# Two attention schedules in one kernel: blocks of 64 tokens for the second sequence, chunks two by two for the first

## The chip, the cores and the metric

The kernel runs on one core of a Trainium2 chip. The metric is device time in microseconds (us) of one execution. Five engines run their own instruction streams and wait for each other by semaphores: PE (TensorE, matmul; PEld is its loading of weights), DVE (VectorE), ACT (ScalarE), POOL (GpSimd) and SP (SyncE), whose queue issues nearly all DMAs.

## The reference

Three stages follow each other: a decayed linear attention, a dense layer with a gelu, and a layer of 8 routed experts.

```python
for b in range(nb):                      # attention: blocks of 64 tokens, head_dim 64
    intra = einsum('bhic,bhjc->bhij', qb, kb) * Dmask      # lam ** (i - j), i >= j
    intra = einsum('bhij,bhjd->bhid', intra, vb)
    inter = einsum('bhid,bhde->bhie', qb * lam_pow, kv_state)
    out[:, :, sl] = intra + inter
    kv_state = lam_block * kv_state + einsum('bhsd,bhse->bhde', kb * rev_pow, vb)
# dense layer on x [1536, 512]
h = x @ w_in                             # w_in [512, 2048]
y = (h * sigmoid(1.702 * h)) @ w_out     # w_out [2048, 512]
# experts
e = argmax(norm(y) @ norm(emb).T / tau)  # one of 8 experts a token, gate = its softmax
out = gate * (relu(y @ w1[e]) @ w2[e])
```

There are 2 sequences of 768 tokens with 8 heads. The size of the attention's blocks does not change what is computed: any block length gives the same sum, split in another way into a part within the block (intra) and a part through the carried state (inter).

## The kernel before

Attention goes in chunks of 128 tokens, six to a sequence (ci 0 to 5 for the first sequence, 6 to 11 for the second), with the 8 heads as 4 pairs, so that two heads of 64 dimensions fill 128 partitions. A chunk has these steps: scores (L228, 8 fp32 matmuls that contract 64 partitions, half of the array each), sm (scores times the mask of decays, DVE L245), kd and qd (k and q scaled by powers of lam, POOL L252 and L258), intra (L279, outputs of 64 columns of the array, half of the array each), inter (L298 for the first sequence, in quarters of the array with the states; L291 for the second, whole array with the state tiles of a pair laid out as a block diagonal, `blocks`), pk (L310, the new part of the state), sd (the old state scaled, ACT L320), state (DVE L329), and the output x as a high part (xh, ACT L342) and a rest (xl, DVE L345). Every fp32 matmul shows as two records in the trace, each with its own loading of weights.

The dense layer runs over 16 hidden blocks f of 128 columns, twice: `emit_moe1_first` for the first sequence, `emit_moe1_last` for the second. A block's weights come as raw 64-bit words, are decoded by three DVE operations (L368, L371, L374) and split into a high half (ACT L386) and a low half (DVE L387); `decode_w(f, kind)` and `split_w(g, f, kind)` are these steps, kind 0 for w_in and 1 for w_out. Then come h (L403, 2 x 12 matmuls into two tiles of 384 tokens), gelu (ACT L414), its split (ACT L424, DVE L425) and y (L446, three matmuls for each of six token tiles of 128, on the block before). In the trace gg is the split gelu, whl the split weights, home the decoded weights and the loaded q, k and v, raw the words as loaded.

Everything stands in a manual schedule: the order of the code is the order of each engine's stream. The first sequence's attention runs ahead of the dense layer (`emit_attention`, a loop over six chunks with loads some chunks ahead). The second sequence's chunks are laid into the y groups of `emit_moe1_first`: with f odd, behind the third group, a chunk's scores, kd, qd and sm (its first place); with f even, behind the second group, all that `chunk_out` does (its second place).

Scores, outputs and pk of the first sequence are in the PSUM pool `psum_y` (6 banks), those of the second in `psum_h` (2 banks), which also holds the two h tiles; a tile that takes a bank waits until its last reader is through.

Of the kernel before, what the change touches and what calls it, by code (L numbers as in the profile page):

```python
# [8 lines left out]
F32 = mybir.dt.float32  # L9
# [8 lines left out]
P = 128  # L18
B, H, S, D = 2, 8, 768, 64
NP = H // 2  # L20
# [29 lines left out]
def attn_moe_moe_kernel(  # L50
# [164 lines left out]
    state = [sp.tile([P, NP, D], F32, tag="junk", name="state")] * B  # L215

    blocks = sp.tile([P, NP, P], F32, tag="junk", name="blocks")


    def psum_a(ci):  # L220
        return psum_y if ci < NC else psum_h

    def emit_scores(ci):
        kq = kqs[ci]
        pair = [psum_a(ci)([P, NP, P], f"sc{ci}_{j}") for j in range(2)]
# [43 lines left out]
    def out_bank(ci):  # L269
        opens = ci not in pos  # L270
        if opens:
            pos[ci] = psum_a(ci)([P, NP, P], f"po{ci}")
        return pos[ci], opens
# [10 lines left out]
    def emit_inter(ci):  # L284
# [4 lines left out]
        for p in range(NP):  # L289
            if ci >= NC:  # L290
                nc.tensor.matmul(  # L291
                    po[:, p, :], blocks[:, p, :], qd[:, p, :],
                    start=(opens and p == 0), stop=True, skip_group_check=True,
                )
                continue
            for j in range(2):
                o = slice(64 * j, 64 * j + 64)
                nc.tensor.matmul(  # L298
                    po[o, p, :], state[ci // NC][o, p, :], qd[o, p, :],
# [3 lines left out]
    def emit_pk(ci):  # L303
# [3 lines left out]
        pk = psum_a(ci)([P, NP, D], f"pk{ci}")  # L307
# [8 lines left out]
    def emit_sd(ci):  # L316
        if 0 < ci % NC < NC - 1:
            sds[ci] = sp.tile([P, NP, D], F32, tag="sq", name=f"sd{ci}", bufs=1)
            for p in range(NP):
                nc.scalar.activation(  # L320
                    sds[ci][:, p], state[ci // NC][:, p], AF.Copy, scale=tq[:, p, P - 1:P]
                )

    def emit_state(ci):
        if ci % NC == NC - 1:
            return
        st, pk = state[ci // NC], pks.pop(ci)
# [4 lines left out]
        if ci >= NC:  # L332
            for j in range(2):
                o = slice(64 * j, 64 * j + 64)
                nc.scalar.activation(blocks[o, :, o], st[o], AF.Copy)

# [7 lines left out]
    def emit_xl(ci):  # L344
        nc.vector.tensor_tensor(  # L345
            x_part(ci, 1), pos.pop(ci), x_part(ci, 0).bitcast(F32), op=ALU.subtract
        )

# [818 lines left out]
    def chunk_out(ci):  # L1167

        if ci >= NC:
            emit_inter(ci)  # L1170
        emit_intra(ci)
        if ci < NC:
            emit_inter(ci)
        emit_pk(ci)
        emit_state(ci)
        emit_xh(ci)
        emit_xl(ci)

    def emit_attention():
# [6 lines left out]
        load_kv(1)  # L1186
        nc.gpsimd.memset(anti, 1.0)
# [7 lines left out]
        nc.gpsimd.memset(blocks, 0.0)  # L1195
# [6 lines left out]
        emit_kd(0)  # L1202
        emit_tq()
# [32 lines left out]
    def emit_moe1_first():  # L1236
        for f in range(NF):
# [5 lines left out]
            if ci and f % 2 and ci + 1 < NCH:  # L1243
                load_kq(ci + 1)
                load_kv(ci + 1)
# [19 lines left out]
            if f == 0:  # L1265
                split_w(0, 0, 1)
# [90 lines left out]
```

## Time and profile before

| | us |
|---|---|
| median of 3 runs | 512.07 |
| lowest, highest | 511.69, 512.15 |
| profiled execution | 511.36 |
| its span in the trace | 509.7 |
| PE busy | 498.2 (98%) |
| DVE busy | 355.6 (70%) |
| ACT busy | 259.5 (51%) |
| POOL busy | 105.2 (21%) |

The span is the time from the first to the last recorded work of the profiled execution; the rest of its 511.36 us lies around it. Busy times are shares of the span and overlap. Matmuls are pipelined and their ends are modelled, so that a record's duration is longer than the distance from its start to the next one's; what a group of matmuls occupies PE for is read from the starts.

### The profile page before, as it was taken

The numbers are of one execution on the slowest core, as the hardware profiler recorded it, in microseconds if no ns is written. First come the engines' busy times: TensorE is split into PE (matmuls) and PEld (weight loads), VectorE is DVE, ScalarE is ACT, GpSimd is POOL, SyncE is SP. The second block draws the span as 40 slices with busy tenths as digits, with TensorE's granted clock in tenths as the row PEclk, the third lists the DMA queues.
The fourth block names the chain that finished last, engine by engine and source line by source line (L and its number), as shares of the span: only waits on it lengthen the run. The fifth ranks groups of instructions, "written<-read, shape, count | busy, mean of one in ns | idle before, by whom it ended". The sixth has DMA issues, their size and how long they took to land. (4 is left out here: it accounts for less than half of the span.)

```text
span 509.7 us, 8519 instructions
## 1 busy us (share of the span) xinstructions
PE 498.2 (98%) x3057; PEld 431.0 (85%) x3058; DVE 355.6 (70%) x838; ACT 259.5 (51%) x546; POOL 105.2 (21%) x144
## 2 busy tenths in 40 slices
PE   8999999999999999999999999999999999999993
PEld 5888898899989998989898998778887988879781
DVE  6888866667676515788879559838967778686640
ACT  2443444343533458443435575537956578666540
POOL 3800110110100012332323229511010111201101
PEclk9999999999999999999999999999999999999997
DMA  8985576764530130111111300259986757865000
GB/s 301 395 324 173 175 245 183 232 206 129 178 108 1 42 127 0 43 62 63 62 63 62 105 18 1 105 193 403 363 295 195 264 180 267 278 216 186 21 10 30
DMA packets 32324, 80.31 MB, mean 158 GB/s; under 512 B 3753, under 2 KB 4265, under 8 KB 32149
## 3 DMA queue, kind: packets, MB, share of 16 engines
q1 hardware_dynamic: 29317, 72.62, 41.8%
q0 software_dynamic: 2240, 6.31, 3.3%
q10 hardware_dynamic: 720, 0.79, 0.6%
q8 instruction: 25, 0.41, 0.3%
q14 instruction: 22, 0.18, 0.1%
HBM read 69.19 MB, written 10.80 MB: 157 GB/s over the span
## 5 line engine op out<-in xcount | busy, mean ns | idle before, releaser
L446 PE MATMUL y<-whl,gg 128*128 128x512 f32 x576 | 141.3, 395 | 0.0
L403 PE MATMUL h<-x,whl 128*128 128x384 f32 x768 | 139.6, 336 | 0.7 <-ACT whl L386 0.6
L403 PEld LDWEIGHTS h<-x,whl 128*128 128x128 f32 x768 | 134.0, 188 | 3.3 <-ACT whl L386 0.9
L446 PEld LDWEIGHTS y<-whl,gg 128*128 128x128 f32 x576 | 106.3, 188 | 21.7 <-issue 0.2
L702 DVE TENSOR_TENSOR wl<-wr,wh 128x1024 fp32r<-128x1024 f32 (+1 forms) x79 | 78.1, 1018 | 5.2 <-ACT wh L697 5.2
L857 PE MATMUL m<-wh,xe 128*128 128x512 f32 (+7 forms) x256 | 80.9, 397 | 0.0
L414 ACT ACTIVATE g<-h 128x384 f32<-128x384 f32 x64 | 31.3, 489 | 77.5 <-PE h L403 75.2
L697 ACT ACTIVATE wh<-wr 128x1024 fp32r<-128x1024 f32 (+1 forms) x79 | 67.3, 890 | 0.0
L821 PE MATMUL m<-xe,wh 128*128 128x464 f32 (+6 forms) x224 | 65.8, 363 | 0.0
L387 DVE TENSOR_TENSOR whl<-home,whl 128x512 fp32r<-128x512 f32 x49 | 34.9, 711 | 41.4 <-ACT whl L386 41.4
L857 PEld LDWEIGHTS m<-wh,xe 128*128 128x128 f32 (+7 forms) x256 | 42.4, 169 | 15.1 <-DVE xe L810 0.2
L386 ACT ACTIVATE whl<-home 128x512 fp32r<-128x512 f32 x64 | 40.0, 626 | 27.1 <-DVE home L374 24.4
L857 PE MATMUL m<-wl,xe 128*128 128x512 f32 (+7 forms) x128 | 50.4, 393 | 0.0
L821 PE MATMUL m<-xe,wl 128*128 128x232 f32 (+6 forms) x224 | 49.8, 262 | 0.0
L425 DVE TENSOR_TENSOR gg<-g,gg 128x384 fp32r<-128x384 f32 x64 | 36.8, 576 | 17.6 <-ACT gg L424 17.4
L512 DVE CUSTOM_DVE_ANT_0 jd<-yr,er 128x512 f32<-128x512 f32 x64 | 48.3, 802 | 0.0
L868 POOL DMA_INDIRECT out<-o,row x16 | 16.9, 1058 | 136.2 <-ACT o L865 85.4
L821 PEld LDWEIGHTS m<-xe,wl 128*128 128x128 f32 x224 | 42.1, 190 | 1.2 <-DVE wl L702 0.3
L387 POOL TENSOR_TENSOR whl<-home,whl 128x512 fp32r<-128x512 f32 x15 | 20.9, 1392 | 101.2 <-ACT whl L386 99.3
L830 DVE TENSOR_TENSOR m1r<-m,m1r 128x232 f32<-128x232 f32 (+6 forms) x56 | 20.7, 370 | 29.0 <-ACT m1r L829 29.0
L821 PEld LDWEIGHTS m<-xe,wh 128*128 128x128 f32 x224 | 39.6, 189 | 1.3
L829 ACT ACTIVATE m1r<-m 128x232 f32<-128x232 f32 (+6 forms) x56 | 19.2, 344 | 35.8 <-PE m L821 33.1
(167 smaller groups left out, 538.4 us busy)
## 6 DMA issues: line engine op xcount, KB each, us to landing
wr<-w SPq DMA_DIRECT2D x64, 512.0 KB, 7.1
raw<-w_in SPq DMA_DIRECT2D x16, 512.0 KB, 3.3
raw<-w_out SPq DMA_DIRECT2D x16, 512.0 KB, 4.3
slots<-zrow SPq DMA_DIRECT2D x8, 514.0 KB, 5.3
sl<-slots SPq DMA_DIRECT2D x7, 514.0 KB, 6.3
home<-vn SPq DMA_DIRECT2D x12, 256.0 KB, 5.1
home<-kT SPq DMA_DIRECT2D x11, 256.0 KB, 5.4
home<-kn SPq DMA_DIRECT2D x11, 256.0 KB, 5.0
```

The source lines that it names most:

```text
L386: nc.scalar.activation(t[:, 0], a, AF.Copy)
L387: eng.tensor_tensor(t[:, 1], a, t[:, 0].bitcast(F32), op=ALU.subtract)
L403: nc.tensor.matmul(t, wt[:, wi, k * P:(k + 1) * P], x[:, xi, k, sl], start=(i == 0), stop=(i == 3 * KD - 1),)
L414: nc.scalar.activation(g2, h1.pop((f, hf)), AF.Gelu_apprx_sigmoid)
L425: nc.vector.tensor_tensor(gl, g2, gh.bitcast(F32), op=ALU.subtract)
L446: nc.tensor.matmul(t, a[:, o:o + P], wt[:, wi], start=(f == 0 and n == 0), stop=(f == NF - 1 and n == 2),)
L512: nc.vector.tensor_tensor_reduce(out=jd, in0=yrow[self.g, self.ts[j]][:, 0:DM], in1=route["er"][:, e], scale=1.0, scalar=0.0, op0=ALU.mult ...
L697: nc.scalar.activation(ws[e, kind, n][0][:, o], wr[e, kind, n][:, o], AF.Copy)
L702: nc.vector.tensor_tensor(l[:, o], wr[e, kind, n][:, o], h[:, o].bitcast(F32), op=ALU.subtract)
L821: nc.tensor.matmul(t[:, 0:n], w[:, fs], x[:, k, 0:n], start=(k == 0 and w is wh), stop=(k == KD - 1 and w is wh),)
L830: nc.vector.tensor_tensor(r, t[:, 0:c], r, op=ALU.add)
L857: nc.tensor.matmul(t[0:n], ht[:, hi_lo, f, off:off + n], w[wi][:, o:o + DM], start=(i == 0), stop=(i == last),)
```

## The change

For the second sequence each chunk now is two blocks of 64 tokens (s = 0 and 1). The tokens of a chunk are stored in reverse order, so block 0 lies in the upper 64 partitions (`rows(s)`). Scores are 16 matmuls of 64x64 with 64 columns, and so are intra and pk; consecutive matmuls of a loop go to different quarters of the array, given by the partitions they contract and those they write. Inter keeps the whole array, as 4 matmuls of 64 columns for each block, with two states and two block diagonals. pk moves from the chunk's second place to its first, beside the scores, and shares their two PSUM banks; kd and the scaled state move to the start of the step f. The state takes two steps a chunk, and DVE's sm two operations of 128x256 instead of 128x512.

For the first sequence the loop over chunks is written out: scores of two chunks one behind the other, then their intra and pk, then inter, with S, I, P and N for scores, intra, pk and inter: S0 S1 I0 P0 S2 S3 I1 P1 I2 P2 N1 N2 S4 S5 I3 P3 I4 P4 I5 N3 N4 N5. Loads are written out too. The constants of POOL come behind the chunks. The decoding of w_out of block 0, which stood ahead of the last chunk's output, stands in step f = 0 now, behind the gelu of the second half.

```diff
+    states = sp.tile([P, 2, NP, D], F32, tag="junk", name="states")
+    scaled = sp.tile([P, 2, NP, D], F32, tag="sq", name="scaled", bufs=1)
...
+    def block_scores(ci):
+        kq = kqs[ci]
+        both = [psum_h([P, 2, NP, C], f"sk{ci}_{j}") for j in range(2)]
+        scores[ci] = [t[:, 0] for t in both]
+        pks[ci] = [t[:, 1] for t in both]
+        for p in range(NP):
+            for s in range(2):
+                for j in range(2):
+                    nc.tensor.matmul(
+                        scores[ci][j][rows(s), p, :],
+                        kq[halves[j], 0, p, rows(s)], kq[halves[j], 1, p, halves[s]],
+                        start=True, stop=True, skip_group_check=True,
+                    )
+    def block_pk(ci):
+        kd = decs[ci][:, 0].rearrange("m (h d) -> m h d", h=H)
+        for p in range(NP):
+            for s in (1, 0) if ci % NC < NC - 1 else (0,):
+                for j in range(2):
+                    nc.tensor.matmul(
+                        pks[ci][1 - s][halves[j], p, :],
+                        kd[rows(s), 2 * p + j, :], kvs[ci][rows(s), 1, 2 * p + j, :],
+                        start=False, stop=True, skip_group_check=True,
+                    )
...
+    def block_sm(ci):
+        sm = chunk_tile(ci, "sm")[:, 0:DM].rearrange("m (j p i) -> m j p i", j=2, p=NP)
+        for j, t in enumerate(scores.pop(ci)):
+            nc.vector.tensor_tensor(sm[:, j], t, mk[:, j, :, 0:C], op=ALU.mult)
+        sms[ci] = sm
...
+    def block_sd(ci, s):
+        n = block(ci, s)
+        if not 0 < n < 2 * NC - 1:
+            return
+        if s:
+            nc.vector.tensor_tensor(
+                scaled[:, 0], states[:, 0], tq[:, :, C - 1:C].to_broadcast([P, NP, D]),
+                op=ALU.mult,
+            )
+            return
+        for p in range(NP):
+            nc.scalar.activation(
+                scaled[:, 0, p], states[:, 1, p], AF.Copy, scale=tq[:, p, C - 1:C]
+            )
+    def block_state(ci, s):
+        n = block(ci, s)
+        if n == 2 * NC - 1:
+            return
+        if n:
+            nc.vector.tensor_tensor(states[:, s], scaled[:, 0], pks[ci][1 - s], op=ALU.add)
+        else:
+            nc.vector.tensor_copy(states[:, s], pks[ci][1 - s])
+        if s == 0:
+            block_copy(0)
...
+    def block_out(ci):
+        pos[ci] = [psum_h([P, NP, C], f"po{ci}_{s}") for s in range(2)]
+        for s in range(2):
+            if block(ci, s):
+                for p in range(NP):
+                    nc.tensor.matmul(
+                        pos[ci][s][:, p, :], blocks[1 - s][p], block_qd_of(ci)[:, p, s, :],
+                        start=(p == 0), stop=True, skip_group_check=True,
+                    )
+        for p in range(NP):
+            for s in range(2):
+                for j in range(2):
+                    nc.tensor.matmul(
+                        pos[ci][s][halves[j], p, :],
+                        kvs[ci][rows(s), 1, 2 * p + j, :], sms[ci][rows(s), j, p, :],
+                        start=(p == 0 and block(ci, s) == 0), stop=True, skip_group_check=True,
+                    )
+        xh, xl = (x_part(ci, i) for i in range(2))
...
+        load_kq(3)
...
-        for ci in range(NC):
-            if ci + 3 < NC:
-                load_kq(ci + 3)
-            if ci + 2 < NC:
-                load_kv(ci + 2)
-            for f, kinds in {1: [(0, (0,))], 3: [(0, (1,))], 4: [(1, (0, 1))]}.get(ci, []):
-                load_w(f, kinds)
-            if ci == 4:
-                load_kq(NC)
-                load_kv(NC)
-            emit_sd(ci)
-            if ci + 1 < NC:
-                emit_sm(ci + 1)
-                emit_qd(ci + 1)
-                emit_kd(ci + 1)
-            if ci == 2:
-                first = decode_ops(0, 0)
-            if 2 <= ci < 5:
-                first[ci - 2]()
-            if ci == NC - 1:
-                split_w(0, 0, 0)
-                decode_w(0, 1)
-            chunk_out(ci)
-            if ci + 2 < NC:
-                emit_scores(ci + 2)
-            if ci == 0:
-                emit_consts_pool()
+        load_kv(2)
+        load_w(0, (0,))
+        for ci in range(4, NC):
+            load_kq(ci)
+        for ci in range(3, NC):
+            load_kv(ci)
+            if ci == 3:
+                load_w(0, (1,))
+        load_w(1)
+        emit_intra(0)
+        emit_pk(0)
+        emit_state(0)
+        emit_xh(0)
+        emit_kd(1)
+        emit_qd(1)
+        emit_scores(2)
+        emit_scores(3)
+        emit_sd(1)
+        emit_sm(2)
+        emit_xl(0)
+        emit_kd(2)
+        emit_qd(2)
+        first = decode_ops(0, 0)
+        for ci in (1, 2):
+            emit_intra(ci)
+            emit_pk(ci)
+            if ci == 1:
+                emit_state(1)
+                emit_sd(2)
+                emit_sm(3)
+        first[0]()
+        emit_inter(1)
+        emit_xh(1)
+        emit_state(2)
+        emit_sd(3)
+        first[1]()
+        emit_xl(1)
+        emit_inter(2)
+        emit_xh(2)
+        emit_kd(3)
+        emit_kd(4)
+        emit_qd(3)
+        emit_qd(4)
+        emit_qd(5)
+        load_kq(NC)
+        load_kv(NC)
+        emit_scores(4)
+        emit_scores(5)
+        emit_sm(4)
+        emit_intra(3)
+        emit_pk(3)
+        emit_sm(5)
+        emit_state(3)
+        emit_sd(4)
+        first[2]()
+        emit_xl(2)
+        emit_intra(4)
+        emit_pk(4)
+        emit_intra(5)
+        emit_inter(3)
+        emit_state(4)
+        split_w(0, 0, 0)
+        emit_xh(3)
+        for ci in (4, 5):
+            emit_inter(ci)
+            emit_xh(ci)
+        for ci in (3, 4, 5):
+            emit_xl(ci)
+        emit_consts_pool()
...
+                block_kd(ci)
+                block_sd(ci, 0)
...
-            if f == 0:
-                split_w(0, 0, 1)
             l1_mm(0, f, 1)
             l1_gelu(0, f, 1)
+            if f == 0:
+                decode_w(0, 1)
+                split_w(0, 0, 1)
...
-                    emit_scores(ci)
-                    emit_kd(ci)
-                    emit_qd(ci)
-                    emit_sm(ci)
+                    block_scores(ci)
+                    block_pk(ci)
+                    block_qd(ci)
+                    block_state(ci, 0)
+                    block_sm(ci)
+                    block_sd(ci, 1)
+                    block_state(ci, 1)
                     if f == 1:
                         decode_next(1)
                     second_half()
                 if ci and f % 2 == 0 and i == 1:
-                    emit_sd(ci)
-                    chunk_out(ci)
+                    block_out(ci)
```

POOL in the first sequence's chunks, from chunk 1 on, before: kd (L252) and qd (L258) of the chunks alternate, home_118 and home_116 being k and v of chunks 3 and 4, home_117, home_115 and home_113 q and k of chunks 3, 4 and 5.

```order
L258 TENSOR_TENSOR dec_282<-home_119,tq 128x512
L252 TENSOR_TENSOR dec_282<-home_120,mask 128x512
L258 TENSOR_TENSOR dec_336<-home_117,tq 128x512
L252 TENSOR_TENSOR dec_336<-home_118,mask 128x512
L258 TENSOR_TENSOR dec_391<-home_115,tq 128x512
L252 TENSOR_TENSOR dec_391<-home_116,mask 128x512
L258 TENSOR_TENSOR dec_450<-home_113,tq 128x512
```

And after (kd is L266, qd is L272):

```order
L266 TENSOR_TENSOR dec_257<-home_123,mask 128x512
L272 TENSOR_TENSOR dec_257<-home_121,tq 128x512
L266 TENSOR_TENSOR dec_288<-home_120,mask 128x512
L272 TENSOR_TENSOR dec_288<-home_119,tq 128x512
L266 TENSOR_TENSOR dec_361<-home_118,mask 128x512
L266 TENSOR_TENSOR dec_363<-home_116,mask 128x512
L272 TENSOR_TENSOR dec_361<-home_117,tq 128x512
L272 TENSOR_TENSOR dec_363<-home_115,tq 128x512
L272 TENSOR_TENSOR dec_367<-home_113,tq 128x512
```

Before, kd of chunk 4 (from home_116) came behind the qd of chunks 3 and 4 (home_117, home_115) and only one qd came behind it; now it stands ahead of all three.

DVE at the end of the first sequence's chunks and in f = 0, before; home_108 is block 0's decoded w_out, home_109 that of block 1, x_126 the output.

```order
L368 TENSOR_SCALAR home_108<-raw_0_381 128x512
L371 SCALAR_TENSOR_TENSOR home_108<-raw_0_381,home_108 128x512
L374 SCALAR_TENSOR_TENSOR home_108<-raw_0_381,home_108 128x512
L345 TENSOR_TENSOR x_126<-po_488,x_126 128x4x128
L368 TENSOR_SCALAR home_109<-raw_1_434 128x512
L371 SCALAR_TENSOR_TENSOR home_109<-raw_1_434,home_109 128x512
L374 SCALAR_TENSOR_TENSOR home_109<-raw_1_434,home_109 128x512
L387 TENSOR_TENSOR whl_1_0_529<-home_109,whl_1_0_529 128x512
L425 TENSOR_TENSOR gg_0_0_532<-g_0_0_0_527,gg_0_0_532 128x384
L387 TENSOR_TENSOR whl_0_1_535<-home_108,whl_0_1_535 128x512
```

And after (xl is L348, decoding L487 to L493, the split L506):

```order
L348 TENSOR_TENSOR x_126<-po_442,x_126 128x4x128
L487 TENSOR_SCALAR home_109<-raw_1_233 128x512
L490 SCALAR_TENSOR_TENSOR home_109<-raw_1_233,home_109 128x512
L493 SCALAR_TENSOR_TENSOR home_109<-raw_1_233,home_109 128x512
L506 TENSOR_TENSOR whl_1_0_527<-home_109,whl_1_0_527 128x512
L544 TENSOR_TENSOR gg_0_0_530<-g_0_0_0_525,gg_0_0_530 128x384
L487 TENSOR_SCALAR home_108<-raw_0_227 128x512
L490 SCALAR_TENSOR_TENSOR home_108<-raw_0_227,home_108 128x512
L493 SCALAR_TENSOR_TENSOR home_108<-raw_0_227,home_108 128x512
L506 TENSOR_TENSOR whl_0_1_551<-home_108,whl_0_1_551 128x512
L487 TENSOR_SCALAR home_109<-raw_1_235 128x512
```

The three operations that decode home_108 moved from ahead of the last chunk's xl to just ahead of its split, behind the first gelu's.

PE in a chunk's second place, before, the chunk 9 within f = 8; po is the output, pk the part of the state.

```order
L446 MATMUL y0_1_613<-whl0_7_1_1120,gg0_7_0_1165 128x512 x3
L291 MATMUL po9_1285<-late_dec_631,blocks_129 128x128 x4
L279 MATMUL po9_1285<-home11_119,home15_123 64x128 x8
L310 MATMUL pk9_1298<-home15_123,late_dec_631 64x64 x8
L446 MATMUL y0_2_617<-whl0_7_1_1120,gg0_7_0_1165 128x512 x3
L446 MATMUL y0_3_644<-whl0_7_1_1120,gg0_7_1_1215 128x512 x3
```

And after, here the chunk 8 within f = 6, up to the first four pairs of intra's matmuls:

```order
L565 MATMUL y0_1_616<-whl0_5_1_1001,gg0_5_0_1051 128x512 x3
L446 MATMUL po8_0_1194<-late_dec_571,scaled_129 128x64 x2
L446 MATMUL po8_0_1194<-late_dec_571,blocks1_131 128x64 x2
L446 MATMUL po8_1_1195<-late_dec_571,blocks0_130 128x64 x4
L453 MATMUL po8_0_1194<-home11_119,home14_122 64x64 x2
L453 MATMUL po8_1_1195<-home11_119,home14_122 64x64 x2
L453 MATMUL po8_0_1194<-home11_119,home14_122 64x64 x2
L453 MATMUL po8_1_1195<-home11_119,home14_122 64x64 x2
L453 MATMUL po8_0_1194<-home11_119,home14_122 64x64 x2
```

Inter has as many matmuls again, with 64 columns instead of 128, intra goes by quarters and pk is gone from this place.

## Rows read from the trace of the kernel before

**Rows 1.** Page, part 1: busy us of each engine, share of the span, instructions

```profile
PE 498.2 (98%) x3057; PEld 431.0 (85%) x3058; DVE 355.6 (70%) x838; ACT 259.5 (51%) x546; POOL 105.2 (21%) x144
```

**Rows 2.** Windows: us, busy by engine (PE PEld DVE ACT POOL), clock, DMA share, GB/s

```profile
20.00:30.00 10.00, 10.00 (x146) 8.69 (x143) 9.64 (x17) 4.57 (x13) 4.40 (x4) 1.00 1.04 402
45.00:150.00 105.00, 105.00 (x710) 93.96 (x709) 74.56 (x133) 43.94 (x96) 11.27 (x9) 1.00 0.61 191
```

**Rows 3.** Timeline of PE: start us, us, engine, line, operation, out<-in, records

```profile
59.03 1.16 PE L228 MATMUL sc<-home 64*128 64x128 f32 x16
60.13 2.35 PE L446 MATMUL y<-whl,gg 128*128 128x512 f32 x9
62.31 4.35 PE L403 MATMUL h<-x,whl 128*128 128x384 f32 x24
...
67.89 1.05 PE L291 MATMUL po<-late_dec,blocks 128*128 128x128 f32 x8
68.88 1.09 PE L279 MATMUL po<-home,home 128*64 128x128 f32 x16
69.80 0.64 PE L310 MATMUL pk<-home,late_dec 128*64 128x64 f32 x16
70.36 3.02 PE L446 MATMUL y<-whl,gg 128*128 128x512 f32 x12
```

**Rows 4.** Timeline of PE, matmuls of 8 columns with whole weights

```profile
316.37 1.85 PE L533 MATMUL pd<-embt,yt 128*128 128x8 f32 x16
318.07 1.41 PE L446 MATMUL y<-whl,gg 128*128 128x512 f32 x5
```

**Rows 5.** Timeline of PE, the stretch of 68.87 to 68.89 us alone

```profile
68.88 0.33 PE L279 MATMUL po<-home,home 128*64 128x128 f32 x2
```

**Rows 6.** Timeline of POOL; in brackets idle us before and what ended them

```profile
16.99 1.27 POOL L258 TENSOR_TENSOR dec<-home,tq 128x512 f32<-128x512 f32 x1
18.22 1.06 POOL L252 TENSOR_TENSOR dec<-home,mask 128x512 f32<-128x512 f32 x1
...
21.06 1.06 POOL L252 TENSOR_TENSOR dec<-home,mask 128x512 f32<-128x512 f32 x1 [0.37 <-DMA home<-kn]
22.08 1.72 POOL L258 TENSOR_TENSOR dec<-home,tq 128x512 f32<-128x512 f32 x1
```

**Rows 7.** Timeline of PE, from the last inter to h of f 2

```profile
26.39 1.09 PE L298 MATMUL po<-dec,state 64*64 64x128 f32 x16
27.41 4.55 PE L403 MATMUL h<-x,whl 128*128 128x384 f32 x24
32.54 4.81 PE L403 MATMUL h<-x,whl 128*128 128x384 f32 x24 [0.59 <-ACT whl L386]
...
42.65 4.35 PE L403 MATMUL h<-x,whl 128*128 128x384 f32 x24
```

**Rows 8.** Timelines of DVE and of ACT, by their starts

```profile
27.53 0.60 ACT L342 ACTIVATE x<-po 128x512 fp32r<-128x512 f32 x1 [1.40 <-PE po L298]
29.01 0.68 DVE L345 TENSOR_TENSOR x<-po,x 128x512 fp32r<-128x512 f32 x1
...
33.60 0.68 DVE L387 TENSOR_TENSOR whl<-home,whl 128x512 fp32r<-128x512 f32 x1
34.20 0.42 DVE L368 TENSOR_SCALAR home<-raw 128x512 uint32<-128x512 uint32 x1
...
36.11 0.63 ACT L386 ACTIVATE whl<-home 128x512 fp32r<-128x512 f32 x1 [2.31 <-DVE home L374]
38.00 0.48 ACT L414 ACTIVATE g<-h 128x384 f32<-128x384 f32 x1
39.76 0.63 ACT L386 ACTIVATE whl<-home 128x512 fp32r<-128x512 f32 x1 [1.29 <-DVE home L374]
...
60.50 1.28 DVE L245 TENSOR_TENSOR home<-sc,mask 128x512 f32<-128x512 f32 x2
```

**Rows 9.** Groups of instructions, shapes apart: xcount | busy us, mean ns | idle before, releaser

```profile
L329 DVE TENSOR_TENSOR state<-sd,pk 128x256 f32<-128x256 f32 x8 | 3.3, 416 | 2.0 <-ACT x L342 1.0 <-PE pk L310 1.0
```

More of the change, by code (lines that the diff above doesn't have):

```diff
@@ L214, in attn_moe_moe_kernel, with rows, block @@
     scores = {}
[L215 to L221, printed above, removed]
+    states = sp.tile([P, 2, NP, D], F32, tag="junk", name="states")
+    scaled = sp.tile([P, 2, NP, D], F32, tag="sq", name="scaled", bufs=1)
+    pieces = [
+        (sp.tile([P, NP, P], F32, tag="junk", name="blocks0"), 0),
+        (scaled[:, 1].rearrange("m (p j) d -> m p (j d)", j=2), 0),
+        (const.tile([P, NP // 2, P], F32, name="blocks1"), 2),
+    ]
+    blocks = [[pieces[0][0][:, p] for p in range(NP)],
+              [t[:, p] for t, _ in pieces[1:] for p in range(NP // 2)]]
+    halves = (slice(0, C), slice(C, P))
+    def rows(s):
+        return halves[1 - s]
+    def block(ci, s):
+        return 2 * (ci % NC) + s
     def emit_scores(ci):
         kq = kqs[ci]
-        pair = [psum_a(ci)([P, NP, P], f"sc{ci}_{j}") for j in range(2)]
+        pair = [psum_y([P, NP, P], f"sc{ci}_{j}") for j in range(2)]
         for p in range(NP):
@@ L289, in emit_inter @@
         for p in range(NP):
[L290 to L295, printed above, removed]
             for j in range(2):
@@ L317, in emit_sd @@
         if 0 < ci % NC < NC - 1:
-            sds[ci] = sp.tile([P, NP, D], F32, tag="sq", name=f"sd{ci}", bufs=1)
+            sds[ci] = scaled[:, 0]
             for p in range(NP):
                 nc.scalar.activation(
-                    sds[ci][:, p], state[ci // NC][:, p], AF.Copy, scale=tq[:, p, P - 1:P]
+                    sds[ci][:, p], states[:, 1 - ci % 2, p], AF.Copy, scale=tq[:, p, P - 1:P]
                 )
@@ L326, in emit_state @@
             return
-        st, pk = state[ci // NC], pks.pop(ci)
+        st, pk = states[:, ci % 2], pks.pop(ci)
         if ci % NC:
@@ L347, in emit_xl, with emit_block_mask @@
         )
+    def emit_block_mask():
+        nc.gpsimd.tensor_copy(mask[halves[0], :, halves[0]], mask[halves[0], :, halves[1]])
+        nc.gpsimd.memset(pieces[1][0], 0.0)
+    def block_scores(ci):
[11 more added lines that the diff above has]
+                    )
@@ new lines, in block_copy @@
+    def block_copy(s):
+        for t, p in pieces[1:] if s else pieces[:1]:
+            w = t.shape[1]
+            for o in halves:
+                nc.scalar.activation(t[o, :, o], states[o, s, p:p + w], AF.Copy)
+    def block_out(ci):
[6 more added lines that the diff above has]
+                        start=(p == 0), stop=True, skip_group_check=True,
+                    )
+        for p in range(NP):
[5 more added lines that the diff above has]
+                        start=(p == 0 and block(ci, s) == 0), stop=True, skip_group_check=True,
+                    )
+        xh, xl = (x_part(ci, i) for i in range(2))
+        for s, o in enumerate(halves):
+            nc.scalar.activation(xh[:, :, o], pos[ci][s], AF.Copy)
+        for s, o in enumerate(halves):
+            nc.vector.tensor_tensor(
+                xl[:, :, o], pos[ci][s], xh[:, :, o].bitcast(F32), op=ALU.subtract
+            )
+        if ci < NCH - 1:
+            block_copy(1)
@@ L1194, in emit_attention @@
         nc.vector.memset(zero_c, 0.0)
-        nc.gpsimd.memset(blocks, 0.0)
+        for t in (pieces[0][0], pieces[2][0]):
+            nc.gpsimd.memset(t, 0.0)
         nc.scalar.activation(warm, zero_c, AF.Gelu_apprx_sigmoid)
```

41 lines of the change are left out of this document (21 added, 20 removed).

## The prediction

> **What bounds the kernel now.** I read the page's busy times first: PE is busy for 498.2 of 509.7 us, DVE for 70% of them, ACT for 51%, POOL for 21% [rows 1]. So a change is worth what it adds to TensorE's stream or takes from it, unless it makes that stream wait. The windows came second. From 45 to 150 us, where the second sequence's chunks lie, PE is busy all the time and DVE for 71% of it; between 20 and 30 us DMA moves 402 GB/s and DVE is busy for 9.64 of 10 us [rows 2]. The granted clock is 1.00 in both, so nothing below is a matter of the clock. What the reader is to see: before about 45 us another engine can set when the dense layer gets on, and behind that only PE's own records count. Third came the timelines of both stretches. The profiled execution took 511.36 us, 0.71 under the median of 512.07; I add up on the former and put the 0.71 on at the end. Below 0.2%, about 1.0 us, a measurement of this kernel can't tell a difference from none.
>
> **Part 1, the chunks of the second sequence.** One fp32 matmul is two records here, lo and hi. Before, a chunk's scores are 16 records of 128 columns and take PE from 59.03 to 60.13, 1.10; its second place takes 67.89 to 70.36, 2.47 [rows 3]. In it, 16 records on half of the array with 128 columns take 69.80 - 68.88 = 0.92, two at a time, 0.115 a step. With 64 columns 16 records take 70.36 - 69.80 = 0.56: eight steps of half the size, 0.46, and 0.10 for going back to the whole array. The 8 whole-array records of inter take 68.88 - 67.89 = 0.99: at 0.106 each (below) that is 0.85, and 0.14 for going over to halves. The scores pay 1.10 - 0.92 = 0.18 for coming and going, so 0.08 for coming.
>
> After, scores and pk stand together: 32 + 32 records of 64 columns, each on a quarter of the array. If four run at once, these are 16 steps of 0.0575, 0.92, and 0.18 for coming and going: 1.10, as before. In the second place inter has 8 matmuls, 16 records with 128x128 weights and 64 columns. No row has that form. From one side: with 8 columns and whole weights a record takes (318.07 - 316.37)/16 = 0.106 [rows 4], so the loading of weights sets it and 64 columns cost the same, 16 x 0.106 = 1.70. From the other: if columns set it, 16 x 0.0575 = 0.92. I take 1.70, since [rows 4] has the same weights and fewer columns still. Then 0.14, 32 quarter records in 8 steps (0.46) and 0.10: 2.40, against 2.47.
>
> That is -0.07 for each of chunks 7 to 10. Chunk 6 has no inter before, 0.08 + 0.92 + 0.46 + 0.10 = 1.56; after, its second block has one, 0.85 + 0.14 + 0.46 + 0.10 = 1.55: nothing. Chunk 11 has no pk before, 2.47 - 0.46 = 2.01; after, the same 2.40: +0.39. (In its first place chunk 11 has 16 records of pk instead of 32, which fit two quarters only, so they take the same 0.46.) Sum over six chunks: -0.28 + 0.39 = **+0.1**.
>
> That four run at once no row shows. What a row shows: two records of a half-array stream have begun within 15 ns of 68.88 [rows 5]. [...] I take four, since that asks for the same step three times over; the other end, two, is a rival below. [...]
>
> The new work of other engines in these places is hidden: DVE operations of 128x256 at 0.416 [rows 9] and ACT copies, with DVE idle for 29% of that stretch. One wait is new: the next L403 takes the bank of the second score tile, free after DVE's third operation there (state, and sm in two halves). Before, the two sm start at 60.50 and this L403 at 62.31 [rows 3, 8]; after, three operations of 0.42 are through by 61.8. That leaves 0.5, so I cost it at nothing; each 0.1 by which DVE came later than that would be 0.6 over six chunks.
>
> **Part 2, the first sequence's chunks.** PE goes through 8 changes of array shape instead of 19; at 0.08 to 0.18 each that is 0.9 to 2.0 us less on PE. It reaches the end only if the last inter comes earlier, and that hangs on POOL. Before, kd of chunk 4 starts at 21.06 on the landing of kn [rows 6]. In SP's queue w_out of block 0 (524,288 bytes) now stands ahead of that kn; at 402 GB/s [rows 2] that is +1.3: kd at 22.35. Behind it POOL has the qd of chunks 3, 4 and 5. kd holds POOL for 22.08 - 21.06 = 1.02, a qd for 18.22 - 16.99 = 1.23 or a little more (1.72 long in one row): the last ends at about 22.35 + 1.02 + 3 x 1.25 = 27.1. Chunk 5's inter, the last of the chunks on PE, 27.41 - 26.39 = 1.02 long, waits for it: the dense layer starts at 28.15 instead of 27.41, **+0.74** [rows 6, 7]. Bounds: if kn landed where it did, POOL would be through at 25.8, and PE 0.6 earlier than before; with 1.72 for each qd it is +2.2.
>
> **Part 3, the put-off decoding.** x hi of chunk 5 starts 0.12 behind inter and takes 0.60, so its x lo comes at 28.15 + 0.72 = 28.87, as before (29.01), since the three operations that decode w_out 0 no longer stand ahead of it on DVE [rows 8]. So all up to 33.60 on DVE stays. There, where DVE's half of the split of w_out 0 stood, these three now come, 36.11 - 34.20 = 1.91 until ACT may start (rows of another block's decoding), and then ACT's split, 0.63: everything behind it on DVE comes **2.54 later** [rows 8]. For ACT, which waits for DVE: the split at 36.11 goes to 38.65 and the gelu of f 1, second half, from 38.00 to 40.54, until 41.02. The second score matmul of chunk 6 needs that gelu's bank, so PE waits there. It waits again for h of f 2: ACT's split of w_in 2 goes from 39.76 to 42.30, ends at 42.93; DVE's half holds DVE for 0.6, until 43.5; then state and the two sm, each 0.42 long but holding DVE for 0.08 less (as 33.60 to 34.20 for one of 0.68): 44.6. Before, this h began at 42.65 [rows 7]: **+2.0**. The 0.74 of part 2 is in it, not beside it: PE stood idle for 0.59 ahead of 32.54 anyway, which takes nearly all of it [rows 7]. From 45 us on PE has no idle time that could give anything back [rows 2].
>
> **Sum.** 511.36 + 2.0 + 0.1 = 513.46; with 0.71 the median is **514.2**.
>
> **Rivals.**
> First, **fewer than four quarters at once**. With two, scores and pk take 32 steps, 1.84 + 0.18 instead of 1.10 (+0.92), intra 16 steps (+0.46). Five chunks at 1.38 and chunk 11 at 0.92 (its pk has two quarters either way) are 7.8, of which 0.4 lies beside DVE's wait in chunk 6: 514.2 + 7.4 = 521.6. For it: no row shows more than two. [...] Three at once would lie near 517. Chance 0.22, with all between.
> Second, **the early part is hidden**: kn lands as early as before, PE's fewer shape changes reach L403, DVE starts on w_in 1 up to 1.9 earlier, and that pays for the put-off decoding. Only the +0.1 is left: 512.2. Against: at 402 GB/s there is no room for half a megabyte more ahead of kn [rows 2]. Chance 0.15.
> Third, the other side: **64 columns make inter cheap**. At 0.0575 a record four chunks save 0.78 each, chunk 6 saves 0.39 and chunk 11 0.78, together 4.3: 514.2 - 4.3 = 509.9. It decides from about 0.08 a record down, where it outweighs the early loss. Against: 8 columns cost 0.106 [rows 4]. Chance 0.10.
>
> **How the numbers follow.** The forecast has 0.53, with a range of its own of 513.0 to 516.0 (below: half a microsecond of part 2's lower bound and of DVE's chain; above: the +2.2 instead of +0.74). Faster by over 0.2%: the third, 0.10. Within 0.2%: the second, 0.15. Slower: 0.53 + 0.22 = 0.75. The range leaves out the third and a little at either end: 511.6 to 522.5.
>
> **What the new profile would show.** The dense layer's first matmul at about 28.15, behind a qd on POOL; PE idle near 40 us and again before h of f 2, at about 44.6; a chunk's first place 1.10 long and its second 2.40, with four records begun within 30 ns. I would be wrong if the quarters took a step of 0.115 for four records, if inter took 0.9, or if h of f 2 started where it did.

## The result, and the profile after

The changed kernel takes 518.18 us (median of 4 runs, 517.85 to 518.38), the kernel before 512.11 in the same comparison (511.69 to 512.70): ratio 1.0118, interval 1.0103 to 1.0134, 6.07 us slower. Forecast were 514.2, or 2.1 slower. The sign is right, and the size is nearly three times as large. 518.18 lies above the forecast's own 513.0 to 516.0; that the wide range up to 522.5 holds it is luck, since that part of it was there for the first rival (fewer than four quarters at once), which is not what happened. The profiled execution took 518.38 us with a span of 516.6, 6.9 more than before. The granted clock was 1.00 from 20 to 150 us in both traces, so the clock has no part in that.

First PE's timeline, in the columns of [rows 3]; after the line in brackets stands idle time and what ended it. L522 is h, L369 the scores, L381 pk, L446 inter, L453 intra, L565 y.

```profile
25.86 3.28 PE L306 MATMUL po<-dec,states 64*64 64x128 f32 x48
29.07 4.43 PE L522 MATMUL h<-x,whl 128*128 128x384 f32 x24
35.69 4.80 PE L522 MATMUL h<-x,whl 128*128 128x384 f32 x24 [2.19 <-ACT whl L505]
40.34 2.25 PE L565 MATMUL y<-whl,gg 128*128 128x512 f32 x9
43.43 0.33 PE L369 MATMUL sk<-home 64*64 64x64 f32 x2 [0.84 <-ACT g L533]
44.36 0.63 PE L369 MATMUL sk<-home 64*64 64x64 f32 x27 [0.61 <-ACT g L533]
...
48.65 4.40 PE L522 MATMUL h<-x,whl 128*128 128x384 f32 x24 [0.85 <-DVE home L405]
...
59.43 4.43 PE L522 MATMUL h<-x,whl 128*128 128x384 f32 x24 [0.57 <-DVE x L462]
...
65.87 0.69 PE L369 MATMUL sk<-home 64*64 64x64 f32 x32
66.39 0.65 PE L381 MATMUL sk<-home,late_dec 64*64 64x64 f32 x32
66.97 2.33 PE L565 MATMUL y<-whl,gg 128*128 128x512 f32 x9
69.14 4.35 PE L522 MATMUL h<-x,whl 128*128 128x384 f32 x24
...
74.71 0.56 PE L446 MATMUL po<-late_dec,scaled 128*128 128x64 f32 x4
...
76.54 0.69 PE L453 MATMUL po<-home,home 64*64 64x64 f32 x32
77.16 3.02 PE L565 MATMUL y<-whl,gg 128*128 128x512 f32 x12
```

Read it against [rows 7] and [rows 3]. h of f 0 starts 1.66 later (29.07 against 27.41), h of f 1 3.15 later (35.69 against 32.54), h of f 2 6.00 later (48.65 against 42.65), and the h at 69.14 6.83 later than the one at 62.31. From there on hardly anything is added (the span grew by 6.9): the loss lies ahead of 70 us. A chunk's first place takes 66.97 - 65.87 = 1.10 and its second 77.16 - 74.71 = 2.45; forecast were 1.10 and 2.40.

Of the scores' records, this many have started within 40 ns of 65.87:

```profile
65.87 0.29 PE L369 MATMUL sk<-home 64*64 64x64 f32 x4
```

Four records did run at once here: the 32 of the scores, each 64x64, took 66.39 - 65.87 = 0.52, where two at a time would have been 16 steps of 0.0575, 0.92 (an estimate with the prediction's step). So the time went elsewhere, and the place to look is DVE's timeline, which I had taken to stay as it was up to 33.60 [rows 8] (L487, L490 and L493 decode, L506 is the split, L348 x lo):

```profile
27.40 1.14 DVE L506 TENSOR_TENSOR whl<-home,whl 128x512 fp32r<-128x512 f32 x1
28.46 2.05 DVE L348 TENSOR_TENSOR x<-po,x 128x512 fp32r<-128x512 f32 x3
30.42 0.70 DVE L487 TENSOR_SCALAR home<-raw 128x512 uint32<-128x512 uint32 x1
31.15 3.04 DVE L490 SCALAR_TENSOR_TENSOR home<-raw,home 128x512 uint32<-128x512 uint32 x1
34.23 0.69 DVE L493 SCALAR_TENSOR_TENSOR home<-raw,home 128x512 uint32<-128x512 uint32 x1
...
46.27 1.24 DVE L506 TENSOR_TENSOR whl<-home,whl 128x512 fp32r<-128x512 f32 x1 [0.23 <-ACT whl L505]
...
55.43 1.82 DVE L506 TENSOR_TENSOR whl<-home,whl 128x512 fp32r<-128x512 f32 x1 [0.23 <-ACT whl L505]
```

One operation that takes 0.69 elsewhere takes 3.04, and no wait is shown for it. POOL's timeline beside it (L272 and L397 qd, L266 and L388 kd):

```profile
23.07 1.25 POOL L266 TENSOR_TENSOR dec<-home,mask 128x512 f32<-128x512 f32 x1 [1.55 <-DMA home<-kn]
24.27 3.72 POOL L272 TENSOR_TENSOR dec<-home,tq 128x512 f32<-128x512 f32 x3
...
31.34 1.05 POOL L388 TENSOR_TENSOR late_dec<-home,mask 128x512 f32<-128x512 f32 x1
32.36 1.28 POOL L397 TENSOR_TENSOR late_dec<-home,tq 128x512 f32<-128x512 f32 x1
45.70 1.26 POOL L388 TENSOR_TENSOR late_dec<-home,mask 128x512 f32<-128x512 f32 x1 [12.06 <-PE sk L381]
55.42 1.29 POOL L397 TENSOR_TENSOR late_dec<-home,tq 128x512 f32<-128x512 f32 x1 [8.46 <-issue]
```

Each long DVE operation ends 0.5 to 0.6 behind a POOL multiplication: 27.99 and 28.54, 33.64 and 34.19, 46.96 and 47.51, 56.71 and 57.25. At 31.34 POOL has two in a row, and DVE's operation, begun at 31.15, ends behind both.

### The profile page after: what moved, and what is told of

Its sections match the earlier page's. It is cut to its first block, busy times and chain, and to the rows that moved or that the text cites. A ratio compares the mean times of both kernels' runs of the same rounds, so it can differ in the third digit from the quotient of the medians.

```text
span 516.6 us, 9240 instructions
## 1 busy us (share of the span) xinstructions
PE 497.7 (96%) x3393; PEld 431.9 (84%) x3394; DVE 359.1 (70%) x855; ACT 267.2 (52%) x578; POOL 108.8 (21%) x149
## 5 line engine op out<-in xcount | busy, mean ns | idle before, releaser
L522 PE MATMUL h<-x,whl 128*128 128x384 f32 x768 | 139.6, 336 | 3.7 <-ACT whl L505 2.2
L565 PE MATMUL y<-whl,gg 128*128 128x512 f32 x576 | 141.3, 395 | 0.0
L522 PEld LDWEIGHTS h<-x,whl 128*128 128x128 f32 x768 | 133.8, 188 | 6.8 <-ACT whl L505 2.5
L565 PEld LDWEIGHTS y<-whl,gg 128*128 128x128 f32 x576 | 106.3, 188 | 21.2
L506 DVE TENSOR_TENSOR whl<-home,whl 128x512 fp32r<-128x512 f32 x49 | 37.1, 756 | 49.8 <-ACT whl L505 49.3
L506 POOL TENSOR_TENSOR whl<-home,whl 128x512 fp32r<-128x512 f32 x15 | 20.9, 1393 | 100.8 <-ACT whl L505 100.8
```

Of the source, the lines that this page charges most:

```text
L506: eng.tensor_tensor(t[:, 1], a, t[:, 0].bitcast(F32), op=ALU.subtract)
L522: nc.tensor.matmul(t, wt[:, wi, k * P:(k + 1) * P], x[:, xi, k, sl], start=(i == 0), stop=(i == 3 * KD - 1),)
L565: nc.tensor.matmul(t, a[:, o:o + P], wt[:, wi], start=(f == 0 and n == 0), stop=(f == NF - 1 and n == 2),)
```

## The experiments

The theory after this: three costs on one chain, DVE's up to h of f 2. POOL's kd and qd of chunk 6 hold up the decoding of w_in 1; the put-off decoding comes on top; and the late kn delays POOL and PE. Rivals: DMAs landing beside DVE; the order of the first sequence on PE; the blocks themselves. Differences below are to the median of the kernel before in the same comparison; ratios are estimated from all runs of it with their spread, and need not be the quotient of the two medians. Lines in a kernel's rows are its own, shifted by its edit.

**e1_act6**, the changed kernel without chunk 6's two multiplications on POOL:

```diff
     def block_kd(ci):
+        if ci == NC:
+            nc.scalar.activation(
+                dec_tile(ci)[:, 0].rearrange("m (h d) -> m h d", h=H), kvs[ci][:, 0], AF.Copy
+            )
+            return
...
     def block_qd(ci):
+        if ci == NC:
+            nc.scalar.activation(
+                dec_tile(ci)[:, 1].rearrange("m (p i) -> m p i", p=NP), kqs[ci][:, 1], AF.Copy
+            )
+            return
```

> This kernel is the changed one, but chunk 6's kd and qd are plain copies on ACT, without their factors of lam, instead of multiplications on POOL (its output is not the reference's for the second sequence). Nothing else moves, the DMAs neither. Theory (POOL's multiplications hold up DVE): the second operation that decodes w_in 1, 3.04 us long in the changed kernel, takes 0.69; h of f 1 starts 2.3 earlier, at 33.4; the median comes to 518.2 - 2.3 = 515.9. Rival (the operation is slow because DMAs land beside it, w_in 2 until 30.8 and w_out 2 until 32.1): it stays near 3.0 long, and the median stays at 518.2.

Measured: 515.51, +3.86 instead of +6.07. DVE's operation, while DMA moved 374 GB/s beside it:

```profile
30.42 0.69 DVE L500 SCALAR_TENSOR_TENSOR home<-raw,home 128x512 uint32<-128x512 uint32 x1
```

It takes 0.69: POOL's multiplications had held it up, and the landings are ruled out (beside the 3.04 of the changed kernel, 31.15 to 34.19, DMA moved 113 GB/s). That the median fell by 2.2 where the theory had 2.3 is in part luck, since this trace differs in three more things. kn landed earlier, and the dense layer started at 28.33 instead of 29.07. The copy of kd now stood on ACT (39.83, 0.61 long) just ahead of the gelu that PE's scores wait for, and that wait was 1.36 instead of 0.84. And TensorE's clock fell, behind that wait and one of 0.61; the last row is in the columns of [rows 2]:

```profile
42.34 1.09 PE L381 MATMUL sk<-home,late_dec 64*64 64x64 f32 x31
43.35 3.41 PE L575 MATMUL y<-whl,gg 128*128 128x512 f32 x9
46.60 4.35 PE L532 MATMUL h<-x,whl 128*128 128x384 f32 x24
...
42.40:45.60 3.20, 3.20 (x43) 2.65 (x37) 2.94 (x9) 1.99 (x4) 1.10 (x1) 0.50 0.04 12
```

The granted clock was 0.50 in this stretch. pk and the y behind it took 46.60 - 42.34 = 4.26; in the changed kernel's chunk 7 they take 69.14 - 66.39 = 2.75. So 1.5 of what the edit gave back was lost again here. The changed kernel's own trace has a wait of 2.19 and no such fall; why it fell in this one is not shown, nor whether it fell in the other three runs.

**e2_gap**, the decoding of w_out 0 where DVE is idle:

```diff
         emit_xl(2)
+        decode_w(0, 1)
         emit_intra(4)
...
             if f == 0:
-                decode_w(0, 1)
                 split_w(0, 0, 1)
```

> This kernel is the changed one, with the decoding of w_out 0 taken out of f 0 again and put where DVE is idle, behind x lo of chunk 2 (23.99 to 27.06). Theory (the put-off decoding costs 2.6 on DVE, of which PE waits 0.84 + 0.61 at the scores of chunk 6 and 0.85 ahead of h of f 2): these 2.3 go, h of f 2 starts at 46.3 instead of 48.65, the median is 515.9. Rival (DVE is late in any case because of POOL, and the decoding lies beside that): h of f 2 moves by less than 0.5, and the median stays above 517.6.

Measured: 517.05, +5.40: only 0.7 came back, and h of f 2 started at 48.38 instead of 46.3. PE's timeline shows where the rest went, again with a row of the windows at the end:

```profile
27.38 1.09 PE L306 MATMUL po<-dec,states 64*64 64x128 f32 x16 [0.51 <-POOL dec L272]
29.05 1.09 PE L306 MATMUL po<-dec,states 64*64 64x128 f32 x16 [0.58 <-POOL dec L272]
30.07 4.44 PE L522 MATMUL h<-x,whl 128*128 128x384 f32 x24
36.71 6.39 PE L522 MATMUL h<-x,whl 128*128 128x384 f32 x24 [2.20 <-ACT whl L505]
42.94 2.25 PE L565 MATMUL y<-whl,gg 128*128 128x512 f32 x9
...
37.80:41.00 3.20, 3.20 (x12) 3.20 (x11) 2.46 (x5) 0.59 (x2) 0.00 (x0) 0.50 0.00 0
```

The decoding now lay beside POOL's three qd, which took 4.80 instead of 3.72, and its last two operations 1.65 and 1.64 instead of 0.69. The dense layer started 1.0 later than in the changed kernel. The scores' waits for the gelu were gone, as expected. Here DVE and POOL delayed each other both ways. The other part is the clock: behind the wait of 2.20 it was granted at 0.50 from 37.80 to 41.00 (what made it fall is not shown), and h of f 1 took 42.94 - 36.71 = 6.23 instead of 40.34 - 35.69 = 4.65, 1.6 more.

**e3_blocks**, the blocks alone; the first sequence's loop, loads, constants and decoding are those of the kernel before:

```diff
-        emit_intra(0)
-        emit_pk(0)
...
+        for ci in range(NC):
...
+            if ci == NC - 1:
+                split_w(0, 0, 0)
+                decode_w(0, 1)
+            chunk_out(ci)
...
+            if f == 0:
+                split_w(0, 0, 1)
             l1_mm(0, f, 1)
             l1_gelu(0, f, 1)
-            if f == 0:
-                decode_w(0, 1)
-                split_w(0, 0, 1)
```

> This kernel has the blocks of 64 for the second sequence as in the changed one, and the first sequence's order, loads, constants and decoding as before the change. Theory (the blocks cost TensorE next to nothing, and what they cost comes from POOL's kd and qd for chunks 6 and 7 beside DVE): chunks' first places 1.10, second places 2.45; decoding of w_in 1 some 0.8 late; the next x lo and h of f 3 some 0.6 late: 512.1 + 0.1 + 1.5 = 513.7. Rival (the blocks are free altogether and all of the loss comes from the first sequence): 512.2. Rival (the blocks are what costs): above 515.

Measured: 514.01, +2.36 (interval of the ratio 1.0036 to 1.0074), nearest the theory. The decoding of w_in 1 had one operation of 1.67 beside kd and qd of chunk 6, although POOL's constants are early here; h of f 1 started 1.49 later than before the change (34.03), not 0.8, and h of f 2 at 44.16.

**e4_wlate**, the load of w_out 0 behind k and v of chunks 4 and 5:

```diff
         for ci in range(3, NC):
             load_kv(ci)
-            if ci == 3:
-                load_w(0, (1,))
+        load_w(0, (1,))
         load_w(1)
```

> This kernel is the changed one, with the load of w_out 0 behind those of k and v of chunks 4 and 5 again. Theory (half a megabyte ahead of kn of chunk 4 holds up POOL's chain and with it the last inter): kn lands at about 21.7 instead of 22.93, the dense layer starts at 27.7 instead of 29.07, the decoding of w_in 1 starts 1.3 earlier; POOL's kd and qd of chunk 6, bound to their own landing at 29.54, then lie beside it in another way and end 1.7 earlier at most; median 516.4 to 516.9. Rival (the start of the dense layer is hidden by DVE's chain): h of f 0 starts 1.3 earlier, and h of f 1 where it did; 518.1.

Measured: 517.22, +5.57, with four runs spread from 515.71 to 518.74; 0.5 gained, less than the theory's 1.3 to 1.8. The dense layer started at 28.34, 0.7 earlier, and DVE's operation still took 3.04. Between the two answers, and with its spread no verdict.

**e5_qdearly**, e2_gap with the qd of chunks 3 to 5 in POOL's idle time:

```diff
         emit_qd(2)
+        emit_qd(3)
+        emit_qd(4)
+        emit_qd(5)
...
         emit_kd(4)
-        emit_qd(3)
-        emit_qd(4)
-        emit_qd(5)
```

> This kernel is e2_gap (w_out 0 decoded where DVE was idle), with the qd of chunks 3, 4 and 5 on POOL ahead of kd of chunk 3 instead of behind kd of chunk 4: q has landed by then, and POOL idles there. Theory (e2_gap gained 0.7 instead of 2.3 because its decoding and POOL's three qd held each other up): the decoding takes 1.9 again instead of 4.0, no inter waits for POOL, the dense layer starts at 29.0 or earlier instead of 30.07; POOL gets to chunk 6's kd when it lands, 29.54, so the decoding of w_in 1 ends at about 33.1 instead of 34.9: against the changed kernel -2.3 and -1.8, median near 514. Rival (the decoding is not what PE waits for): as e2_gap, 517.

Measured: 514.65, +2.44, 3.0 less than e2_gap. The decoding of w_out 0 took 0.68, 0.69 and 0.70 for its operations, and the dense layer started at 28.25, 1.8 earlier than in e2_gap: the collision is what had delayed it there. But the 3.0 are not the collision alone, for the clock is 1.00 from 20 to 60 us here, and e2_gap's low clock was 1.6 of them. A new wait came in, 0.67 ahead of h of f 2: DVE's split took 1.59 beside chunk 7's kd.

**e6_pklate**, e5_qdearly with chunk 4's pk behind the inters of chunks 3 and 4 on PE:

```diff
         emit_intra(4)
-        emit_pk(4)
         emit_intra(5)
         emit_inter(3)
+        emit_inter(4)
+        emit_pk(4)
         emit_state(4)
         split_w(0, 0, 0)
         emit_xh(3)
-        for ci in (4, 5):
-            emit_inter(ci)
-            emit_xh(ci)
+        emit_xh(4)
+        emit_inter(5)
+        emit_xh(5)
```

> This kernel is e5_qdearly, and on PE the inters of chunks 3 and 4 stand ahead of chunk 4's pk, so that only this pk and the last inter are behind the landing of kn of chunk 4. Theory (the late kn holds up a queue of work on PE that does not need it): the dense layer starts at about 27.0, 2 us earlier; the decoding of w_in 1 starts near 28.5 and meets chunk 6's kd and qd only with its last operation; h of f 1 at 32, h of f 2 near 42.3; median 512.0 to 512.8. Rival (DVE's chain, not PE, sets h of f 1, and POOL's kd and qd meet it wherever it lies): 514.

Measured: 513.93, +1.72. The mechanism was wrong: the dense layer started at 29.54, not 27.0, since the last inter then waited 0.59 for the state behind pk, and PE had waited longer for landings of q (1.7 in all, against 0.6 in e5_qdearly). h of f 2 started at 44.89.

**e7_putoff**, e6_pklate with the decoding back in f 0, as in the change.

> This kernel is e6_pklate with the decoding of w_out 0 in f 0 again, as in the changed kernel. It prices the put-off decoding by itself, with POOL out of its way. Theory: everything on DVE behind it 2.6 later, PE waits at the scores of chunk 6 and ahead of h of f 2; 2.0 to 2.6 over e6_pklate. Rival (the put-off decoding lies in time that DVE has anyway): within 0.5 of e6_pklate.

Measured: 516.68, +4.47, 2.75 over e6_pklate. PE's rows have the change's waits again, although the dense layer started a microsecond earlier than in e6_pklate:

```profile
41.53 0.32 PE L369 MATMUL sk<-home 64*64 64x64 f32 x2 [0.84 <-ACT g L533]
42.47 0.63 PE L369 MATMUL sk<-home 64*64 64x64 f32 x27 [0.61 <-ACT g L533]
...
46.75 1.46 PE L522 MATMUL h<-x,whl 128*128 128x384 f32 x7 [0.87 <-DVE home L405]
```

So the price of the put-off decoding is 2.75, near the 2.54 that part 3 had for DVE, and more than its 2.0 for PE.

**e8_both**, e6_pklate with e4_wlate's loads.

> This kernel is e6_pklate with the load of w_out 0 behind those of k and v of chunks 4 and 5 as well. Theory: kn of chunk 4 lands 0.9 to 1.3 earlier, the dense layer starts near 26.2; w_out 0 lands at about 24.2, its decoding ends at 26.2 and does not hold up anything; h of f 2 by 0.5 earlier than in e6_pklate: 511.3 to 512.3. Rival (from here on landings of w_in 1 and of chunk 6 set the time): as e6_pklate.

Measured: 513.97, +1.76: as e6_pklate, the rival's answer. kn of chunk 4 landed early enough for its kd to start at 21.41, but the dense layer started at 28.07, not 26.2, and PE still waited 1.37 ahead of h of f 1: decoding w_in 1 had operations of 1.27 and 1.67 beside chunk 6's kd and qd.

**e9_blocks_act6**, e3_blocks with e1_act6's edit.

> This kernel is e3_blocks with chunk 6's kd and qd as plain copies on ACT, without their factors, as in e1_act6 (its output for the second sequence is not the reference's). Theory (of the blocks' 2.4 over the kernel before, about 1.0 to 1.5 is POOL beside the decoding of w_in 1, the rest the same with chunk 7 and the spread of the landings): 0.1 to 1.2 over the kernel before on the same chip, 512.2 to 513.3. Rival (the blocks themselves cost TensorE that much): 514.

Measured: 511.94 against 511.84, ratio 0.9999 (0.9988 to 1.0011). The blocks cost nothing that can be told where POOL keeps off the decoding of w_in 1; that is the low end of the theory's 0.1 to 1.2. PE's rows ahead of h of f 1 and f 2:

```profile
32.49 4.81 PE L532 MATMUL h<-x,whl 128*128 128x384 f32 x24 [0.27 <-ACT whl L515]
...
42.58 0.69 PE L532 MATMUL h<-x,whl 128*128 128x384 f32 x3
```

Both stand where they stood before the change [rows 7].

**e10_swap** and **e11_swap_ipn** looked for a version better than both, from the kernel before:

```diff
             if ci == NC - 1:
                 split_w(0, 0, 0)
-                decode_w(0, 1)
+                decode_w(1, 0)
...
-            decode_next(0)
+            if f:
+                decode_next(0)
+            else:
+                decode_w(0, 1)
```

and for e11_swap_ipn also

```diff
         emit_intra(ci)
+        emit_pk(ci)
         if ci < NC:
             emit_inter(ci)
-        emit_pk(ci)
...
+                emit_kd(ci + 1)
                 emit_qd(ci + 1)
-                emit_kd(ci + 1)
```

> This kernel is the one before the change, with one edit: ahead of the last chunk's output DVE decodes w_in of block 1 instead of w_out of block 0, and w_out 0 follows in f 0 where w_in 1 stood. Theory (in the kernel before PE waits 0.59 ahead of h of f 1 for w_in 1, and w_out 0 is wanted only some 4 us later): the 0.59 goes, 0.4 to 0.6 under the kernel before. Rival (the split of w_out 0 or the gelu becomes late instead): no difference, or up to 0.5 over it.

> This kernel is e10_swap, and in the first sequence's chunks pk stands right behind intra (the same tile shape) and ahead of inter, one change of shape less a chunk; POOL has kd ahead of qd for that. One chunk at a time otherwise, so that no chunk waits for the next one's loads. Theory (the changes of shape are worth 0.1 to 0.15 each where PE does not wait for landings): the dense layer starts at 26.7 to 26.9 instead of 27.41, in all 0.9 to 1.2 under the kernel before. Rival (PE waits for kd, as it did for 0.34 once): as e10_swap or worse.

Measured: 511.38 and 511.41 against 511.84, ratios 0.9998 (0.9981 to 1.0016) and 0.9992 (0.9978 to 1.0007): no difference that can be told. The medians lie 0.46 and 0.43 lower, but three runs of twelve and one of twelve lie at 513.9 to 514.5. In the profile of e10_swap PE waited 0.62 at h of f 1 as before, now for DVE: decoding had met chunk 6's kd (1.18 for an operation of 0.42). In that of e11_swap_ipn the dense layer started at 28.07, not 26.7 to 26.9: PE had waited 0.54 for POOL's qd, much as its rival had it for the kd. No version tried is shown to beat the kernel before.

**e12_order_alone**, e5_qdearly with e1_act6's edit; of the change's early costs the order two by two is left, with POOL's qd out of its way.

> This kernel is e5_qdearly with chunk 6's kd and qd as plain copies on ACT, without their factors (its output for the second sequence is not the reference's). Of the change's costs only the first sequence's order two by two is left: the decoding is back, POOL's qd are out of the way, POOL's multiplications no longer lie beside the decoding of w_in 1, and the blocks cost nothing (e9_blocks_act6). Theory (PE saves 11 changes of shape, and waits at the scores and at chunk 4's pk for landings, since two chunks have to be there at a time): the dense layer starts at 28.0 to 29.0 instead of 27.41, 0.5 to 1.5 over the kernel before. Rival (the order is free, the rest of the loss is still POOL or DVE): within 0.3 of the kernel before.

Measured: 512.17 against 511.95, ratio 0.9999 (0.9987 to 1.0011). My theory (0.5 to 1.5) fell; the rival (within 0.3) held. PE's rows:

```profile
25.39 2.88 PE L306 MATMUL po<-dec,states 64*64 64x128 f32 x48
28.20 8.85 PE L532 MATMUL h<-x,whl 128*128 128x384 f32 x48
```

The dense layer starts 0.8 late, but h of f 1 follows h of f 0 without a gap; before, there was one of 0.59. By h of f 2, at 42.51 (before: 42.65), PE has made the late start good. Behind it PE waits 0.58 at h of f 3 for chunk 6's x lo, as in the changed kernel (0.57).

## Why the prediction was wrong

**Part 1 (chunks) was right**: 1.10 and 2.45 measured for 1.10 and 2.40, inter with 64 columns at the rate of 8 columns (76.54 - 74.71 = 1.83 for 1.70 + 0.14), scores with four records at once (32 in 0.52); e9_blocks_act6 puts the sum at 0.1. The rivals of two quarters and of a cheap inter are out. [rows 5] have two begun together, so that four would be was the prediction's estimate; the trace of the changed kernel has four begun within 40 ns.

**The step that failed is part 3's "So all up to 33.60 on DVE stays".** It counted DVE's own operations and left out what else the change moved beside them. Before, chunk 6's kd stood alone there, and met one operation of the decoding, 0.76 long instead of 0.42:

```profile
29.03 1.06 POOL L252 TENSOR_TENSOR late_dec<-home,mask 128x512 f32<-128x512 f32 x1 [5.23 <-DMA home<-kn]
...
29.61 0.76 DVE L368 TENSOR_SCALAR home<-raw 128x512 uint32<-128x512 uint32 x1
```

Now POOL's constants went behind the chunks, this kd behind them, and a qd, which chunk 6 did not need before, behind the kd, so that POOL multiplied from 31.34 to 33.64, just while DVE decoded w_in 1, which PE waits for next. The prediction took "the new work of other engines in these places" as hidden and named only DVE's and ACT's. One operation of the decoding took 2.35 longer by it (3.04 instead of 0.69). In the median it is 2.2 us from e5_qdearly to e12_order_alone (2.44 and 0.22), and 2.3 in the blocks alone, from e3_blocks to e9_blocks_act6 (2.36 and 0.10). A smaller piece of the same kind is the 0.57 at 59.43: DVE's split of 1.82 beside chunk 7's qd delays the x lo whose bank h of f 3 takes. The margin of part 1 spoke of the first place only.

**The put-off decoding** was sized right for DVE: 2.54 there, 2.63 in the trace (the split of w_out 0 moved from 33.60 to 39.38, that of w_in 1 only from 32.52 to 35.67), 2.75 measured in the time (e6_pklate to e7_putoff). The waits it named are the ones that the trace shows (0.84, 0.61, 0.85). But for PE it had 2.0 at h of f 2, and that needed a DVE that is on time ahead of it.

**Part 2**: the dense layer came 1.66 later, not 0.74. kn of chunk 4 let kd start at 23.07, not 22.35; in e1_act6, whose loads are the same, at 22.32. So the landing is right to within how landings vary between executions, and so is the path: POOL's last qd ends at 27.99, and the dense layer starts 1.08 behind it, about an inter's length (1.02). A start 0.8 late costs nothing on its own (e12_order_alone, where the qd are early), because PE's idle time ahead of h of f 1 takes it; 1.66 was not tried alone. With DVE late for other reasons it counts in full, about 0.8 of the 3.15 at h of f 1 (the decoding of w_in 1 starts at 30.42 instead of 29.61). Part 2 said that it lay inside the 2.0, which needed a DVE that was on time.

The sum as it stands: 2.2 for POOL beside DVE, 2.75 for the put-off decoding, and a remaining 1.1 for the late start with the smaller collision. These prices come from kernels in which other edits stood already, and they overlap: e1_act6 gave back 2.2 although 1.5 went to the clock, so that POOL's term taken out of the changed kernel alone would be nearer 3 (an estimate: 2.2 + 1.5, less 0.7 for the earlier landing). What makes up the 1.1 was not tried singly (e4_wlate's spread is too wide); from the changed kernel to e7_putoff, which has the three qd early and chunk 4's pk late, the difference is 6.07 - 4.47 = 1.6.

## What to carry to other kernels

List what every engine does beside the critical chain after the move, not only what stands in the chain: moving POOL's work cost nearly as much as moving the chain's own operations (2.2 and 2.75). A delay that hides in an idle gap while it is alone counts once another delay has used the gap (the start 0.8 late cost nothing in e12_order_alone and, as estimated above, about 0.8 in the changed kernel), so price them together. When an undo gains less than its price, look for what it met in its new place before dropping the theory: e2_gap's decoding was worth 2.75, and showed 0.7. And when an undo gains just its price, look at the trace all the same, the granted clock included: e1_act6's 2.2 was a sum of four things.

## What the runs showed of the hardware

In these runs some operations of DVE and POOL were longer beside each other than alone: 3.04 instead of 0.69 for one that decodes in the changed kernel, 4.80 instead of 3.72 for POOL's three qd in e2_gap. It stood in the trace of before, in rows that I had not read for it; DVE's (POOL's kd and qd run there until 22.12 and from 22.08 to 23.80, [rows 6]):

```profile
21.61 1.06 DVE L371 SCALAR_TENSOR_TENSOR home<-raw,home 128x512 uint32<-128x512 uint32 x1
22.59 0.41 DVE L329 TENSOR_TENSOR state<-sd,pk 128x256 f32<-128x256 f32 x1
22.92 0.68 DVE L345 TENSOR_TENSOR x<-po,x 128x512 fp32r<-128x512 f32 x1
```

The decoding, with two inputs from SBUF, took 1.06 instead of 0.69, and the qd beside it 1.72 instead of 1.27, the one row that I had taken for scatter; x lo, with one input from PSUM, took its usual 0.68. Two inputs from SBUF are not the whole of it: the first operation of the decoding has one, and it too was long beside POOL (0.42 elsewhere; 0.76 before, in the rows above, 1.18 in e10_swap, 1.27 in e8_both). What makes them long is not shown. Nor does it follow from the recorded starts which of the two is longer. In e12_order_alone DVE's split began at 40.63, just ahead of chunk 7's kd at 40.69, and took 0.69, while the kd took 1.55. In the changed kernel DVE's operation began at 31.15, ahead of the kd at 31.34, and it was DVE's that was longer, by 2.35, and ended behind both multiplications; the same row is 3.04 long in e2_gap and e4_wlate.
